# Two recurrent attention layers and two gated layers: per-head weight products formed on chip, and both layers advanced in one stream of segments

## The chip, the cores and the metric

The kernel runs on one core of one Trainium2 chip. The metric is the device time of one execution in microseconds, median of several runs; lower is better. The engines are PE (TensorE, matrix products), DVE (VectorE), ACT (ScalarE), POOL (GpSimd) and SP (which issues transfers); in the traces below each starts its instructions in the order in which the program put them there, and stands at one whose inputs or outputs are not free, whatever stands behind it.

## The reference, cut to what matters

```python
def A(x, mem0, Wq, Wk, Wv, Wo):            # 16 heads of 256, model width 448
    mem = mem0                              # 8 memory rows
    for s in range(64):                     # segments of 32 rows, one after the other
        h = concat([mem, x[32*s:32*s+32]])  # 40 rows
        q, k, v = h@Wq, h@Wk, h@Wv          # per head
        p = softmax(where(mask, q@k.T/16, -1e9))
        o = sum over heads of (p@v)@Wo
        mem = o[:8]                         # the next segment needs it
        outs.append(o[8:])

def B(x): return (relu(x@W_gate) * (x@W_up)) @ W_down      # 448 -> 1792 -> 448

x = x + A(layernorm(x)); x = x + B(layernorm(x))
x = x + A(layernorm(x)); x = x + B(layernorm(x))            # same weights again
```

Both attention layers use the same weights, and so do both gated layers (GLU below). Within a layer the memory makes segment s+1 wait for segment s. But layer 2's segment s needs only layer 1's segment s (and the GLU of it), so the two layers can run at the same time, some segments apart.

## The kernel before

It runs layer A, then B, then A, then B. In A, the projections of 128 ordinary rows (four segments) are computed ahead as filler; what depends on the memory is computed in each segment, 8 columns at a time:

```python
def step(self, s):                       # one segment of one layer
    # q and k of the 8 memory rows, after the previous segment's memory
    for qk in range(2):
        for blk in range(32):
            for kt in range(4):
                matmul(psA[:, c*8:c*8+8], lhsT=W[kt, blk], rhs=memT[kt])     # 128x128 by 128x8
    ...                                  # filler: projections of the next four segments
    for h in range(16): ...              # scores, softmax
    for r_ in range(2):                  # v of the memory rows: four column tiles side by side
        for jj in range(4):
            for kt in range(4):
                matmul(psO[r_][32*jj:32*jj+8, 0:512], lhsT=memT[kt], rhs=Wv[kt, chunk],
                       tile_position=(0, 32*jj))
    ...                                  # transposes of P, P@V, evictions
    for dc in range(4):                  # the new memory: 8 columns again
        for blk in range(32):
            matmul(psA[:, dc*8:dc*8+8], lhsT=Wo[blk, dc], rhs=OmT[blk])
```

## Time and profile before

| | |
|---|---|
| time | 4356 us |
| PE / DVE / ACT busy | 79% / 19% / 22% |
| mean granted PE clock | 0.71 |
| matmuls | 75,328, of them 49,152 of 8 columns |

The page's first part lists the busy time of each engine, its share of the span and its instructions; the fourth part follows the work that ended last back through whatever released each step.

```profile
PE 3462.1 (79%) x75328; PEld 2657.6 (61%) x75328; DVE 838.8 (19%) x2249; ACT 972.6 (22%) x2144; POOL 4.8 (0%) x8
...
PE 74%; DMA 8%; ACTq 8%; ACT 6%; DVE 2%; issue 2%; SPq 0%; DVEq 0%
```

PE is the bottleneck, and it is mostly busy. What with? The groups of PE instructions (line, operation, output and inputs, shapes and count | busy us, mean ns of one | idle before, and what ended it):

```profile
L726 PE MATMUL psA<-memT,Wqk_sb 128*128 128x8 bf16 x8192 | 875.9, 168 | 0.0
L594 PE MATMUL psB<-xnT,Wqk_sb 128*128 128x128 bf16 x2048 | 529.6, 259 | 0.0
L726 PE MATMUL psA<-memT,Wk_sb 128*128 128x8 bf16 x12288 | 452.7, 168 | 2.1 <-issue 2.0
L907 PE MATMUL psA<-arena,Wo_sb 128*128 128x8 bf16 x16384 | 449.4, 167 | 12.3 <-ACT arena L879 12.0 <-issue 0.3
L726 PE MATMUL psA<-memT,Wq_sb 128*128 128x8 bf16 x12288 | 448.5, 168 | 24.4 <-DVE memT L920 24.4
```

The groups of L726 and L907 have means of 167 or 168 ns, but these matmuls overlap in the pipeline: the cost of one is the spacing from one start to the next. In the windows view (us from the start; length, busy time and number, granted clock, transfers) 256 matmuls of 8 columns take 7.0 us and 128 of them 3.35 us, 26 to 27 ns each. The clock in the longer stream is half (0.50), yet one matmul costs nearly the same there as in the shorter one at full clock:

```profile
1002.19:1009.18 6.99, 6.99 (x257) 0.50 0.02 5
1022.96:1026.31 3.35, 3.35 (x130) 1.00 0.02 5
1077.78:1080.16 2.38, 2.38 (x39) 0.80 0.00 0
```

So an 8-column matmul costs about half of a 128-column one at full clock (16 of those take 1.06 us; less about 0.17 us until the last one's result is out, its drain, that is 55 ns each). The third window is the column-tiled V product: 32 matmuls of 512 columns in 2.4 us at clock 0.80. One after the other at that clock they would take about 8.8 us (an estimate: 4 x 55 ns each, divided by 0.80), so the four tiles run side by side. The Trainium skill ("TensorEngine Tiling (Array Packing)", Theoretical Speedup) gives up to 4 times for this, and the trace agrees with about 3.7 times.

Four segments of one layer take 116 us, 29 us a segment, 128 times; the two GLU stages take 257 and 251 us, loading 57 us.

### The profile page before, as it was taken

To read this page: it belongs to the slowest core of one execution; us is meant where nothing else is said; L and a number is where in the kernel's file an instruction comes from. 1 tells how busy PE (TensorE), PEld (TensorE's weight loads), DVE (VectorE), ACT (ScalarE), POOL (GpSimd) and SP (SyncE) were. 2 spreads that over 40 slices of the span, in tenths; PEclk is the share of its full clock that TensorE was granted. 3 is DMA by queue.
4 is the path that set the end of the run, shared out by engine and by line. 5 is a ranking of instruction groups with operands and counts; after the bars stand their busy time and mean duration, and the time that the engine had idled before them with its cause. 6 is when DMAs were issued, how large, how long until landed. Compare 5 with 4: busy or idle time off the path is not lost.

```text
span 4355.4 us, 157049 instructions
## 1 busy us (share of the span) xinstructions
PE 3462.1 (79%) x75328; PEld 2657.6 (61%) x75328; DVE 838.8 (19%) x2249; ACT 972.6 (22%) x2144; POOL 4.8 (0%) x8
## 2 busy tenths in 40 slices
PE   2888888888888888866668888888888888888567
PEld 2766666666666667642246666666666666666333
DVE  2111111111111111112221111111111111111132
ACT  1222222222222222212222222222222222221122
POOL 0000000000000000000000000000000000000000
PEclk8677677767776677667776667767777777676588
DMA  4000000000000000010010000000000000000100
GB/s 158 13 14 17 16 17 17 16 16 14 16 17 15 15 17 12 17 43 28 17 31 15 16 12 17 14 17 16 17 17 16 17 17 14 16 17 16 55 17 13
DMA packets 57597, 94.70 MB, mean 22 GB/s; under 512 B 13376, under 2 KB 49728, under 8 KB 51520
## 3 DMA queue, kind: packets, MB, share of 16 engines
q1 hardware_dynamic: 44672, 76.25, 6.7%
q10 hardware_dynamic: 12288, 8.40, 1.1%
q8 instruction: 590, 9.67, 0.9%
q14 instruction: 47, 0.39, 0.0%
HBM read 35.33 MB, written 7.34 MB: 10 GB/s over the span
## 4 chain that ended last, share of the span: by engine, by line
PE 74%; DMA 8%; ACTq 8%; ACT 6%; DVE 2%; issue 2%; SPq 0%; DVEq 0%
PE psA L726 20%; PE psB L594 12%; PE psA L907 10%; PE psO L777 8%; ACTq L805 8%; PE psB L661 6%; PE psB L624 5%; DMA xring<-out_dram 3%; PE psO L861 3%; PE psO L982 2%; PE psS L758 2%; ACT arena L801 2%; DMA arena<-arena 2%; PE psB L982 2%; DMA out_dram<-xring 1%
## 5 line engine op out<-in xcount | busy, mean ns | idle before, releaser
L726 PE MATMUL psA<-memT,Wqk_sb 128*128 128x8 bf16 x8192 | 875.9, 168 | 0.0
L726 PEld LDWEIGHTS psA<-memT,Wqk_sb 128*128 128x128 bf16 x8192 | 843.7, 103 | 0.4 <-issue 0.2
L594 PE MATMUL psB<-xnT,Wqk_sb 128*128 128x128 bf16 x2048 | 529.6, 259 | 0.0
L603 ACT ACTIVATE arena<-psB 128x512 bf16<-128x512 f32 x512 | 299.1, 596 | 838.1 <-PE psB L594 570.2
L726 PEld LDWEIGHTS psA<-memT,Wq_sb 128*128 128x128 bf16 x12288 | 446.3, 102 | 35.6 <-DVE memT L920 27.4
L726 PE MATMUL psA<-memT,Wq_sb 128*128 128x8 bf16 x12288 | 448.5, 168 | 24.4 <-DVE memT L920 24.4
L907 PEld LDWEIGHTS psA<-arena,Wo_sb 128*128 128x128 bf16 x16384 | 446.1, 101 | 25.5 <-ACT arena L879 16.5
L907 PE MATMUL psA<-arena,Wo_sb 128*128 128x8 bf16 x16384 | 449.4, 167 | 12.3 <-ACT arena L879 12.0
L726 PE MATMUL psA<-memT,Wk_sb 128*128 128x8 bf16 x12288 | 452.7, 168 | 2.1 <-issue 2.0
L726 PEld LDWEIGHTS psA<-memT,Wk_sb 128*128 128x128 bf16 x12288 | 444.1, 104 | 2.4 <-issue 2.4
L594 PE MATMUL psB<-xnT,Wq_sb 128*128 128x128 bf16 x3072 | 324.7, 253 | 111.4 <-ACT arena L603 74.6
L594 PE MATMUL psB<-xnT,Wk_sb 128*128 128x128 bf16 x3072 | 344.3, 262 | 72.6 <-ACT arena L603 72.6
L777 PE MATMUL psO<-Wv_sb,memT 128*8 128x512 bf16 x4096 | 365.6, 518 | 0.0
L624 PE MATMUL psB<-Wv_sb,xnT 128*128 128x512 bf16 x1024 | 292.0, 425 | 76.9 <-ACT arena L635 76.9
L594 PEld LDWEIGHTS psB<-xnT,Wq_sb 128*128 128x128 bf16 x3072 | 256.3, 115 | 146.1 <-ACT arena L603 79.7
L594 PEld LDWEIGHTS psB<-xnT,Wk_sb 128*128 128x128 bf16 x3072 | 269.8, 119 | 106.6 <-ACT arena L603 77.7
L737 ACT ACTIVATE arena<-psA 128x512 bf16<-128x512 f32 x128 | 76.4, 597 | 954.7 <-PE psA L726 954.7
L861 PE MATMUL psO<-arena 40*128 40x40 bf16 x4096 | 141.5, 188 | 153.4 <-DMA arena<-arena 153.4
L661 PE MATMUL psB<-Wo_sb,arena 128*128 128x448 bf16 x1024 | 249.2, 413 | 0.0
L594 PEld LDWEIGHTS psB<-xnT,Wqk_sb 128*128 128x128 bf16 x2048 | 245.8, 120 | 0.0
L861 PEld LDWEIGHTS psO<-arena 40*128 40x128 bf16 x4096 | 128.2, 100 | 180.4 <-issue 164.4
L777 PEld LDWEIGHTS psO<-Wv_sb,memT 128*8 128x8 bf16 x4096 | 128.1, 104 | 168.1 <-issue 138.1
(90 smaller groups left out, 2479.1 us busy)
## 6 DMA issues: line engine op xcount, KB each, us to landing
arena<-arena SPq DMA_DIRECT2D x128, 256.0 KB, 2.9
arena<-arena ACTq DMA_DIRECT2D x512, 16.0 KB
out_dram<-xring SPq DMA_DIRECT2D x64, 112.0 KB, 1.7
xring<-out_dram SPq DMA_DIRECT2D x64, 112.0 KB, 2.0
Wo_sb<-in_A_Wo_dram SPq DMA_DIRECT2D x1, 3584.0 KB, 36.1
xring<-in_A_x_dram SPq DMA_DIRECT2D x32, 112.0 KB, 1.9
arena<-in_B_W_down_dram SPq DMA_DIRECT2D x2, 1568.0 KB, 12.6
Wq_sb<-in_A_Wq_dram SPq DMA_DIRECT2D x3, 1024.0 KB, 9.4
```

What stands on the lines that cost most here:

```text
L594: r = sch.emit("pe", lambda E, ci=ci, kt=kt, lhsT=lhsT, rhs=rhs: E.matmul(ps[:, ci * 128:(ci + 1) * 128], lhsT=lhsT, rhs=rhs, start=(kt == ...
L603: te = sch.emit("act", lambda E: E.activation(dst, src, ACT.Copy), waits=[(ev_p, tl), qkt_wait_pe], inc=ev_a)
L624: r = sch.emit("pe", lambda E, kt=kt, lhsT=lhsT, rhs=rhs: E.matmul(ps[:, 0:512], lhsT=lhsT, rhs=rhs, start=(kt == 0), stop=(kt == 3)), wai ...
L661: r = sch.emit("pe", lambda E, blk=blk: E.matmul(ps[:, 0:D], lhsT=S.OsT[oi][:, blk, :], rhs=S.Wo_sb[:, blk, :], start=(blk == 0), stop=(bl ...
L726: r = sch.emit("pe", lambda E, c=c, kt=kt, lhsT=lhsT, rhs=rhs: E.matmul(S.psA[:, c * 8:c * 8 + 8], lhsT=lhsT, rhs=rhs, start=(kt == 0), st ...
L758: r = sch.emit("pe", lambda E, base=base, col=col, cq=cq, ck=ck, et=et: E.matmul(S.psS[base:base + L, col:col + L], lhsT=S.QKT[wi][:, cq, ...
L777: rr = sch.emit("pe", lambda E, r_=r_, jj=jj, kt=kt, lhsT=lhsT, rhs=rhs: E.matmul(S.psO[r_][32 * jj:32 * jj + 8, 0:512], lhsT=lhsT, rhs=rh ...
L801: te = sch.emit("act", lambda E, r_=r_: E.activation(S.vstage[0:104, r_, :], S.psO[r_][0:104, 0:512], ACT.Copy), waits=[(ev_p, t_vm[r_]), ...
L805: tvm = sch.emit("act", lambda E, jj=jj: E.dma_start(dstv[:, :, jj, :], S.vstage[32 * jj:32 * jj + 8, :, :]), waits=[(ev_a, t_vmev[1]), (e ...
L861: r = sch.emit("pe", lambda E, pi=pi, i=i, blk=blk, h=h: E.matmul(S.psO[pi][:, L * i:L * i + L], lhsT=S.Vbuf[vb][0:L, blk * 128:blk * 128 ...
L907: r = sch.emit("pe", lambda E, dc=dc, d0=d0, blk=blk: E.matmul(S.psA[:, dc * 8:dc * 8 + 8], lhsT=S.Wo_sb[:, blk, d0:d0 + 128], rhs=S.OmT[: ...
L982: r = sch.emit("pe", lambda E, ps=ps, kt=kt, lhsT=lhsT, rhs=rhs: E.matmul(ps[:, 0:ntok], lhsT=lhsT, rhs=rhs, start=(kt == 0), stop=(kt == 3)),
```

## The change

The intent: fold weights that are only ever used together. Scores are h (Wq Wk^T) h^T and the output is P h (Wv Wo), per head. M = Wq Wk^T and N = Wv Wo (448 x 448 per head) are formed once on chip. Then one product T = M h serves scores, V disappears (P multiplies h itself), and N is applied at the end. All 40 columns of a segment, memory and ordinary rows, go through T together, and layer 2's segment, four behind, joins them as 40 more columns. The GLU takes 64 rows of each layer as one tile of 128. Everything is issued in one loop of 68 steps, with `run_fill` putting the output product (even steps) or the GLU (odd steps) between the parts of the recurrence. The diff is a rewrite; its core, cut and shortened (names such as `m_nat` and `p_t_mem` stand for blocks of the kernel):

```diff
-for qk in range(2):                          # per segment and layer
-    for blk in range(32):
-        for kt in range(4): matmul(psA[:, 8 cols], W[kt, blk], memT[kt])
-... Q/K of four segments: 64 x 4 matmuls of 128 columns, V: 32 of 512
-for dc in range(4):
-    for blk in range(32): matmul(psA[:, 8 cols], Wo[blk, dc], OmT[blk])
+LAG = 4                                      # layer 2 is four segments behind
+def layers(t): return (0 if t < 64 else 1, 2 if t >= LAG else 1)
+# setup, once: transposes of Wq, Wk, Wv, then per head M = Wq Wk^T, N = Wv Wo
+def t_unit(t, k, r, eng):                    # 7 units of 8 blocks in each step
+    for j in range(8):
+        for kt in range(4):
+            MM(R[r][:, j, both layers], M[:, kt, 8*k+j, :], hT[kt, both layers])   # 80 columns
+    ...                                      # two evictions, on ACT or DVE in turn
+def un_mem(t):                               # memory rows of both layers times N
+    for k in range(14):
+        for j in range(4):                   # four column tiles
+            MM(b[32*j:32*j+32, 0:448], UTm[:, 14*j+k : 14*j+k+2], N[:, 14*j+k], ...)
+    hi = copy(b)  (ACT);  lo = b - hi  (DVE) # two bf16 halves of the new memory
+def ln_stats(...):                           # per layernorm
+    bn_stats, bn_aggr (DVE); Ln, Exp (ACT)
+def step(t):
+    side = [m_nat] + ([ln_b] if odd) + softmax ops of t-1 + [transposes of P]
+    for k in [6, 0, 1, 2, 3, 4, 5]:
+        t_unit(t, k, ...); two of side
+    fill = even: projections of t-1, then U N of the pair;  odd: GLU of the last pair
+    run_fill(500); s_mem(t); s_seg(t); run_fill(1500); p_t_mem; run_fill(400); u_mem
+    odd: rest of the GLU, then fill = projections of t-1, statistics of the next pair
+    un_mem(t); ...; run_fill(1200); m_t(t); ...; run_fill(rest)
```

## The prediction

> **What bounds the kernel now.** TensorE. The busy table gives PE 79% of 4355 us, DVE 19%, ACT 22%; the chain that ended last is 74% PE. Attention is 87% of the time: in the timeline four segments of one layer take 116 us, 29 us a segment, 128 times = 3.7 ms; two GLU stages about 0.5 ms; loading 57 us. Much of the PE work is tiny: 49,000 of 75,000 matmuls have 8 columns (256 for memory Q/K and 128 for the new memory per segment, 7.0 and 3.35 us, 26 ns each). In the windows view the clock is 0.50 inside the Q/K streams, 1.00 inside wide ones, mean 0.71; matmuls of 128 columns take 55 ns (16 in 1.05 us) at full clock, 107 at half. The Trainium skill ("TensorE: Matmul & The Clock Gate", Part 1) knows the states 4/8 and 8/8, chosen by how busy the array is; the trace agrees.
>
> **Removed, added.** Matmuls by the instruction order: 75,328 to about 31,000. Gone: the Q/K and V projections (4 + 256 + 32 per group), 384 8-column matmuls per segment, V staging DMAs, phase barriers. Added per step (both layers at once, 68 steps): 224 matmuls of 80 columns, 56 column-tiled of 448, about 75 small; per pair of steps 56 of 448 columns plus GLU 112 of 128 and 14 of 448. At full clock (55 ns per 128 columns; column tiling overlaps fourfold, 32 of 512 in 2.4 us): 8.0 + 2.8 + about 3.5, and 19.5/2 = 9.8 us: 24 us of PE per step, about 1.65 ms in all. Products on chip: transposes and evictions (0.6-1.1 us each), prologue about 115 us instead of 57.
>
> **Critical path.** PE will not be dense: in-order queues make new waits, summed with trace durations (evict 512: 0.69 DVE, 0.60 ACT; reduce/add 320: 0.49; stats 0.63; ACT table load 1.28):
> - odd steps: the GLU's layernorm sits after 34 matmuls of the step; statistics plus Ln and Exp, each with its table load, 3.1 us on ACT, stall PE about 6 us.
> - odd steps, end: the next layernorm's Ln/Exp and loads stand before the hi copy of the new memory on ACT; then lo, projection evictions, transposes: about 6-7 us stall.
> - transpose of P, first PSUM bank after the last T unit, hB before the down projection, U before the output product: 1-2.5 us each.
> Even step about 31 us, odd about 42, 73 per pair; 34 pairs, the first and last two lighter, is 2.45 ms. Plus prologue and tail. Stalls over 3 us also drop the clock. DVE work is about 16 us, ACT 13 us per step.
>
> **Predicted: 2560 us**, 80% range 2230 to 2880. Faster by over 2%: 0.98; within 2%: 0.01; slower: 0.01.
>
> **What would show it.** About 31,000 matmuls; PE busy 60-75%; T matmuls the costliest group, 36 ns each; mean clock 0.8-0.95; table loads about 136; PE idle before the GLU transposes (bG<-xn) near 6 us per pair released by DVE's normalisation; DVE about 45% and ACT about 35% busy; a pair of steps at 73 us, odd longer than even; T start after prologue near 115 us.
>
> **What would make it wrong.** If stalls keep the clock at half, T units cost 67 ns per matmul and the time nears 3 ms. If 80-column streams count as busy and the waits overlap more than my serial sum, 2.2 ms. If column-tiled 448-column matmuls do not overlap, +7 us per step, 0.5 ms.

## The result, and the profile after

The changed kernel takes 2521.5 us (2515.6 to 2522.3, 4 runs), the kernel before 4356.5; the ratio is 0.578 (95% interval 0.577 to 0.579). Ratios here are the mean time of one kernel's runs over that of the other's of the same rounds, so not quite the ratio of the medians quoted. The predicted time was 2560, 1.5% off. It computes the reference.

Busy times and the chain of the changed kernel:

```profile
PE 1940.4 (77%) x30924; PEld 1399.6 (56%) x30924; DVE 1074.5 (43%) x2630; ACT 861.8 (34%) x1859; POOL 94.3 (4%) x160
...
PE 59%; DVE 24%; ACT 13%; issue 4%; POOL 0%; DVEq 0%; ACTq 0%; POOLq 0%
```

PE's share of the span hardly changed, but the chain did: 37% of it is DVE and ACT, where it was 8%. The groups:

```profile
L126 PE MATMUL R<-hT,Mw 128*128 128x80 bf16 (+1 forms) x15232 | 653.5, 212 | 45.2 <-issue 23.1
...
L126 PE MATMUL bO<-Nw,big 128*128 128x448 bf16 x1904 | 437.9, 386 | 62.5 <-DVE big L294 61.2
...
L126 PE MATMUL bC<-Nw,UTm 128*32 128x448 bf16 x3752 | 194.6, 359 | 1.4 <-DVE UTm L294 1.4
L126 PE MATMUL bG<-ident,xn 128*128 128x128 bf16 x272 | 39.4, 297 | 193.8 <-DVE xn L507 193.8
```

The last line is 68 sets of four small transposes with 194 us of idle PE before them: nearly all of it is the GLU's layernorm, once per odd step. One even step, one odd step and the pair, in the windows view (columns: length, busy time and count of PE, PEld, DVE, ACT and POOL, PE clock, transfers):

```profile
1362.82:1395.73 32.91, 28.56 (x411) 18.80 (x412) 11.78 (x29) 7.87 (x20) 0.00 (x0) 0.90 0.01 1
1395.73:1434.53 38.80, 27.02 (x491) 21.64 (x490) 18.84 (x45) 16.40 (x33) 2.22 (x4) 0.86 0.02 5
1362.82:1434.53 71.71, 55.59 (x901) 40.44 (x902) 30.62 (x74) 24.28 (x53) 2.22 (x4) 0.88 0.01 3
```

A pair of steps moves both layers on by two segments each, with all their GLU work, in 71.7 us. The kernel before needed 4 x 29 us for the attention alone. 16 us of the pair PE is idle. Adding up PE's gaps of over 0.2 us over the steady steps: 4.4 us in an even step (1.9 before the output product, 1.5 before the transposes of P, 0.95 before the projections), 11.9 in an odd one (5.7 before the GLU's transposes, 3.1 before the late projections, 0.6 to 0.9 in four other places).

The longest of these in the timeline (start us, length, engine, line, operation, count; in brackets the idle time before it and what ended it):

```profile
1324.01 1.31 PE L126 MATMUL R<-hT,Mw 128*128 128x80 bf16 x32
1324.21 0.62 DVE L780 TENSOR_TENSOR XB<-bO,XA 128x448 bf16<-128x448 f32 x1 [4.40 <-PE bO L126]
...
1326.94 0.63 DVE L496 BATCH_NORM_STATS2 stat<-XB 128x6 f32<-128x448 bf16 x1
1327.00 0.54 ACT L292 ACTIVATE hK<-bC 8x448 bf16<-8x448 f32 x1 [0.89 <-DVE hK L294]
1327.56 1.28 ACT L498 ACT_TABLE_LOAD   x1
1327.60 0.18 DVE L497 BATCH_NORM_AGGREGATE stat<-stat 128x2 f32<-128x6 f32 x1
1328.85 0.29 ACT L498 ACTIVATE stat<-stat,cvec 128x1 f32<-128x1 f32 x1
1329.17 1.28 ACT L500 ACT_TABLE_LOAD   x1
1330.46 0.20 ACT L500 ACTIVATE stat<-stat 128x1 f32<-128x1 f32 x1
1330.77 0.61 DVE L507 TENSOR_SCALAR xn<-XB,stat 128x448 bf16<-128x448 bf16 x2 [2.98 <-ACT stat L500]
...
1331.43 0.61 PE L126 MATMUL bG<-ident,xn 128*128 128x128 bf16 x4 [5.73 <-DVE xn L507]
```

PE has 192 more T matmuls of this step to run, but the transposes stand before them in its queue. They wait for DVE's normalisation, that for ACT's Exp, that for a table load, Ln, another table load and DVE's statistics.

### The profile page after: what moved, and what is told of

The parts are those of the page before. It is cut to its first block, busy times and chain, and to the rows that moved or that the text cites. A ratio compares the mean times of both kernels' runs of the same rounds, so it can differ in the third digit from the quotient of the medians.

```text
span 2520.5 us, 67762 instructions
## 1 busy us (share of the span) xinstructions
PE 1940.4 (77%) x30924; PEld 1399.6 (56%) x30924; DVE 1074.5 (43%) x2630; ACT 861.8 (34%) x1859; POOL 94.3 (4%) x160
## 4 chain that ended last, share of the span: by engine, by line
PE 59%; DVE 24%; ACT 13%; issue 4%; POOL 0%; DVEq 0%; ACTq 0%; POOLq 0%
PE R L126 28%; PE bO L126 21%; PE bC L126 6%; DVE big L294 5%; DVE TTs L294 4%; ACT L500 3%; PE bG L126 3%; ACT TTs L292 2%; ACT L498 2%; DVE xn L507 2%; DVE TTm L294 1%; DVE hK L294 1%; DVE hB L800 1%; DVE stat L657 1%; DVE Ps L659 1%
## 5 line engine op out<-in xcount | busy, mean ns | idle before, releaser
L126 PE MATMUL R<-hT,Mw 128*128 128x80 bf16 (+1 forms) x15232 | 653.5, 212 | 45.2 <-issue 23.1
L126 PEld LDWEIGHTS R<-hT,Mw 128*128 128x128 bf16 x15232 | 639.3, 108 | 76.2 <-issue 38.6
L126 PE MATMUL bO<-Nw,big 128*128 128x448 bf16 x1904 | 437.9, 386 | 62.5 <-DVE big L294 61.2
L126 PEld LDWEIGHTS bO<-Nw,big 128*128 128x128 bf16 x1904 | 188.0, 105 | 260.7 <-DVE big L294 67.2
L126 PE MATMUL R<-xBT,big 128*128 128x128 bf16 x3808 | 232.7, 220 | 28.2 <-ACT TTs L292 27.5
L126 PEld LDWEIGHTS R<-xBT,big 128*128 128x128 bf16 x3808 | 215.9, 98 | 33.9 <-ACT TTs L292 31.8
L126 PE MATMUL bC<-Nw,UTm 128*32 128x448 bf16 x3752 | 194.6, 359 | 1.4 <-DVE UTm L294 1.4
L126 PE MATMUL bG<-ident,xn 128*128 128x128 bf16 x272 | 39.4, 297 | 193.8 <-DVE xn L507 193.8
L294 DVE CAST TTs<-R 128x512 bf16<-128x512 f32 (+3 forms) x272 | 177.0, 651 | 0.0
L294 DVE CAST big<-R 128x512 bf16<-128x512 f32 (+1 forms) x256 | 146.9, 618 | 53.7 <-PE R L126 50.8
L292 ACT ACTIVATE TTs<-R 128x512 bf16<-128x512 f32 (+3 forms) x272 | 153.2, 563 | 0.0
```

The costliest lines, as they stand in the source:

```text
L126: ins = E.matmul(out, lhsT=lhsT, rhs=rhs, **kw)
L292: self.sc.op("act", lambda E: E.activation(out, src, ACT.Copy), reads, writes)
L294: self.sc.op(eng, lambda E: E.tensor_copy(out, src), reads, writes)
```

## The experiments

Eight kernels ran; all of them computed the reference. Ratios are to the kernel before (the changed kernel: 0.578).

### 1. The products without the common stream (e1_no_stream)

```diff
-LAG = 4
+LAG = 64          # layer 2 starts when layer 1 has ended; its input goes through DRAM
```

(with the loads and stores that this needs). The per-head products, T, U and N, the column tiling and all orders stay; each of 128 steps now has one layer in it.

> Products kept, but layer 2 is 64 segments behind instead of 4 (its input goes through DRAM), so the layers run one after the other: 128 steps of one layer instead of 68 of mostly two. Theory A (my prediction's arithmetic: a step costs almost the same for one layer as for two, since T falls only from 36 to about 25 ns a matmul and the waits stay): the one-layer steps at the end of the changed kernel's trace take 31 us, so about 128 x 32 + 170 = 4250 us, range 4000 to 4600: the gain is nearly all lost. Rival B (the products are the gain, fewer matmuls per layer): well below, 3000 to 3500 us.

It took 3945 us, ratio 0.906: below theory A's range (layer 1's steps took 30.7 us on average and layer 2's 28.9, not 32), and far above rival B's. So of the 1835 us that the change took off, the products and the new shape of a step bring 410 alone, and running both layers at once 1425. Why it is so much is in the page's first line of this run, and in 96 T matmuls of 40 columns in its timeline (first line of the second block) against 96 of 80 in that of the changed kernel (second line):

```profile
PE 3185.3 (81%) x54316; PEld 2200.5 (56%) x54316; DVE 1485.4 (38%) x4429; ACT 1259.5 (32%) x3057; POOL 161.7 (4%) x280
```

```profile
1261.38 2.56 PE L126 MATMUL R<-hT,Mw 128*128 128x40 bf16 x96
...
1371.24 3.60 PE L126 MATMUL R<-hT,Mw 128*128 128x80 bf16 x96
```

1245 of the 1425 us are PE busy time, at nearly the same mean clock (0.875 here, 0.879 there). A T matmul of 40 columns (less the drain: 25 ns) costs two thirds of one of 80 (36 ns); and the output product and the GLU multiply a tile of 128 rows whether 64 or 128 of them mean something. Sharing work, more than filling waits, is what the stream does. In this form: a kernel with one layer at a time could fill those tiles with 128 rows of its own layer, so 410 us may not be all that the products can bring alone; that was not tried.

### 2. One table set for Ln and Exp (e2_one_table)

```diff
 def _(eng):
+    eng.preload_act_table_set("natural_log_exp_and_others")
     for f in ops["act"]: f(eng)
```

The Trainium skill ("ScalarE: Activation LUTs", Table sets: the hidden batching unit) says that one named set holds both functions, so that Ln followed by Exp needs one load. The trace of the changed kernel shows that this does not come by itself: both the Ln and the Exp of each of 68 layernorms have a load of 1283 ns.

> One line: a table set that holds both Ln and Exp is loaded once, so 136 table loads of 1.28 us go. Theory A (the layernorm chains of the odd steps hold PE, tables are 2.56 us of each): PE idle before the GLU's transposes 5.7 to about 3.2 us per pair, idle before the late projections 3.1 to about 1 us, 4.5 to 5 us per pair, 2340 to 2380 us. Rival B (ACT is 34% busy, its loads are hidden, DVE's chain sets the wait): under 1 us per pair, 2490 to 2520.

It took 2398 us, ratio 0.551, with one load left. This lies between the two theories' numbers, nearer to A. The idle before the GLU's transposes fell from 5.7 to 3.4 us a pair, as expected (117.0 us in all, from 193.8):

```profile
L126 PE MATMUL bG<-ident,xn 128*128 128x128 bf16 x272 | 32.2, 253 | 117.0 <-DVE xn L508 117.0
```

The idle before the late projections fell only from 3.1 to 2.1, not to 1. The timeline of the changed kernel says why: there the first of the two loads runs long before its input is there, at 1350.59, while ACT waits for DVE's statistics until 1356.27, so only the second load was on that path.

```profile
1350.59 1.28 ACT L498 ACT_TABLE_LOAD   x1
...
1356.05 0.18 DVE L497 BATCH_NORM_AGGREGATE stat<-stat 128x2 f32<-128x6 f32 x1
1356.27 0.29 ACT L498 ACTIVATE stat<-stat,cvec 128x1 f32<-128x1 f32 x1 [4.39 <-DVE stat L497]
1356.58 1.28 ACT L500 ACT_TABLE_LOAD   x1
...
1357.88 0.20 ACT L500 ACTIVATE stat<-stat 128x1 f32<-128x1 f32 x1
1357.98 0.53 ACT L712 ACTIVATE hi<-bC 128x448 bf16<-128x448 f32 x1
```

### 3. The GLU's transposes later on PE (e3_lnb_late)

```diff
-side = [m_nat, ln_b (statistics, apply, transposes), softmax ops, seg_pt]
+side = [m_nat, ln_b (statistics, apply), softmax ops, seg_pt, ln_b_t (transposes)]
```

> Only the GLU layernorm's transposes are moved on PE from after 34 matmuls to after the transposes of P; its Ln and Exp with the loads stay where they are. Theory A (the early place in PE's order is the cause): idle before these transposes 5.7 to under 0.5 us; ACT still stands 3 us in the loads while T waits for evictions, so 2.5 to 5 us per pair come back, 2350 to 2440 us. Rival B (the next wait, transposes of P or T's banks, takes all of it): 2490 to 2520.

It took 2466 us, ratio 0.566: 56 us less, outside both ranges. The idle before the transposes went to 0.5 us as theory A said, but PE then stood before the third T unit instead:

```profile
L126 PE MATMUL R<-hT,Mw 128*128 128x80 bf16 (+1 forms) x15232 | 667.2, 214 | 185.3 <-DVE TTs L294 141.2 <-issue 22.8 <-ACT hT L292 13.6
```

T's second bank is emptied by DVE, and that eviction stands behind the normalisation in DVE's queue, which still waits for ACT's Exp. Taking the wait off PE's queue moved it to DVE's: T's own idle rose from 0.7 to 5.0 us a pair of steps.

### 4. Both (e4_table_late)

> Both. Theory A: the two causes overlap only in the GLU chain, so 5.7 plus about 2 us per pair less, 2230 to 2290 us, mean clock above 0.90 [...]. Rival B (what one of them leaves hides the other): no better than the better of the two alone.

It took 2346 us, ratio 0.539, not the 2230 to 2290 of theory A. The saving of 176 us is about the sum of the two alone (123 and 56). It is better than either alone, so rival B is out too. T still waits 2.8 us in each pair of steps: 68.9 us in all are ended by the same eviction on DVE, which now stands behind a shorter chain.

```profile
L126 PE MATMUL R<-hT,Mw 128*128 128x80 bf16 (+1 forms) x15232 | 622.9, 207 | 116.9 <-DVE TTs L295 68.9 <-ACT hT L293 23.8 <-issue 23.1
```

### 5. The memory's output product without column tiles (e5_no_coltile)

```diff
-for k in range(14):
-    for j in range(4):
-        MM(b[32*j:32*j+32, 0:D], UTm[:, 14*j+k : 14*j+k+2], N[:, 14*j+k], ...)
+for o in range(56):
+    MM(b[0:16, 0:D], UTm[:, o], N[:, o], start=(o == 0), stop=(o == 55))
```

(with the selection matrices to match: one block of rows instead of four).

> The output product of the memory rows runs as 56 matmuls of 16 stationary columns one after another in one column tile instead of four tiles side by side (same result). Theory A (tiles overlap fourfold and the product lies on the chain of every step): 56 x 189 ns = 10.6 us instead of 2.8, about 7.5 us more in each of 67 steps, 3000 to 3060 us. Rival B (tiles hardly overlapped, or the product hides under waits): under 2700 us.

It took 3008 us, ratio 0.690: 487 us more, 7.3 us in each of 67 steps, as theory A had it. The 56 matmuls take 2.83 us in four tiles (the changed kernel's timeline, first line) and 10.76 us in one (this run's):

```profile
1386.69 2.83 PE L126 MATMUL bC<-Nw,UTm 128*32 128x448 bf16 x56
...
1646.43 10.76 PE L126 MATMUL bC<-Nw,UTm 128*16 128x448 bf16 x56
```

Of the 7.9 us that the product became longer, 7.3 show in the step, so hardly any of it vanishes in waits elsewhere. At 487 us the column tiling of this one product is worth more than the waits that runs 2 to 4 removed (176 us).

### 6. Order alone (e6_order)

On top of run 4, no instruction is added or removed. What moved, and the one dependency that was loosened (last line):

```diff
 def step(t):
-    side: two per T unit, in the order m_nat, ln_b, softmax, seg_pt
+    odd:  [m_nat] [statistics, reduce] [Ln/Exp, subtract] [exp, sum, apply] [1/x, P] [seg_pt, ln_b_t] []
+    even: [m_nat, reduce] [subtract, exp] [sum, 1/x] [P] [] [seg_pt] []     # one list per T unit
-    run_fill(500); s_mem(t)
+    s_mem(t); run_fill(500)
+    odd: two projections before the last of the down projection, not after un_mem
+    odd: statistics and apply of the next pair both before un_mem's hi and lo; run_fill(300), not 1200, after un_mem
-un_units: each waits for all of U                     # a dependency, not only an order
+un_units: each waits only for the chunk of U that it reads
```

> On top of one table and late transposes only the order in which work is put into the in-order queues changes: GLU statistics, Ln/Exp and normalisation spread over the T units, transposes of P one or two units later, the memory's scores before the first projection, two late projections before the end of the down projection, the next normalisation before hi/lo, the output product waiting only for the chunk of U it reads. Theory A (the remaining idle of PE, about 12 us a pair, is mostly order): T's bank wait 2.8 to under 1, late projections 2.2 to under 0.7, U 1.9 to under 0.5, P 2.2 to about 1: 6 to 7 us per pair, 2100 to 2170 us. Rival B (DVE's 16 us per step and the serial chain set the pace): over 2280 us.

It took 2076 us, ratio 0.476, a little better than theory A and the fastest of all. Against run 4, which it builds on, that is 269 us or 11.5% less; against the changed kernel 445 us, but 176 of these are run 4's. The page and one pair of steps:

```profile
PE 1823.2 (88%) x30924; PEld 1315.8 (63%) x30924; DVE 1065.9 (51%) x2630; ACT 689.1 (33%) x1723; POOL 94.3 (5%) x160
```

```profile
1130.81:1158.89 28.08, 25.90 (x411) 17.27 (x412) 11.79 (x30) 8.18 (x21) 0.26 (x1) 1.00 0.01 2
1158.89:1188.26 29.37, 25.26 (x491) 19.93 (x490) 18.42 (x45) 11.00 (x28) 1.96 (x4) 0.99 0.03 6
1130.81:1188.26 57.45, 51.16 (x901) 37.20 (x902) 30.20 (x75) 19.17 (x49) 2.23 (x5) 0.99 0.02 4
```

Set against the changed kernel's pair (so with run 4's part in it), matmuls and DVE work are the same; 14.3 us are gone, of them about 10 us idle PE and 4.4 us of PE busy time, the same matmuls at clock 0.99 instead of 0.88. DVE with the same work as before does not hold the kernel above 2280 us, as rival B had it. In the odd step shown T waits 0.3 us in all, the wait of the late projections is gone, and 1.8 us now stand before the selection of the new memory (it waits for lo). The moves were made together; which of them brought how much is not shown.

### 7. Useless matmuls in the wait (e7_keep_warm)

Runs 2 to 6 mix two effects: a changed amount of waiting, and a higher clock (0.90 to 0.97, from 0.88). This run adds work to the changed kernel to separate them.

```diff
+    # odd steps, after m_nat, before ln_b: into a bank that the next T unit overwrites
+    for j in range(96): MM(R[1][...], M[:, 0, j % 8, :], hT[0, both layers], start=True, stop=True)
```

> The changed kernel with 96 useless 80-column matmuls (3.4 us) put into PE's idle 5.7 us before the GLU's transposes in odd steps. Theory A (the idle drops the clock to half for 3 us afterwards and that costs about 1.5 us a pair): clock 0.50 after the wait becomes 1.00 and the time falls by 30 to 60 us, to 2460 to 2490. Rival B (after the wait DVE and ACT set the pace, PE's clock does not matter there): 2510 to 2530.

It took 2514 us, ratio 0.576. The number fits rival B, but the run did not do what it was made for: the windows after the useless matmuls show that the clock fell to 0.50 all the same, as soon as the transposes came. So it says nothing about what the half clock costs.

```profile
1395.78:1397.78 2.00, 1.13 (x32) 1.00 (x28) 0.00 (x0) 1.97 (x3) 0.00 (x0) 1.00 0.03 8
1397.78:1399.78 2.00, 0.58 (x12) 0.58 (x13) 0.61 (x2) 0.79 (x3) 0.00 (x0) 0.97 0.00 0
1399.78:1401.78 2.00, 2.00 (x34) 2.00 (x32) 0.15 (x1) 0.46 (x1) 0.00 (x0) 0.50 0.00 0
```

The gap left was 2.3 us. The Trainium skill ("TensorE: Matmul & The Clock Gate", the table at its end) asks for no gaps over about 3 us; here 2.3 us was already too long. So was less: in an even step of the changed kernel the 1.92 us before the output product (from 1306.29 to 1308.21) ended in the half clock too, and the clock records of the whole trace show it after each of the 32 waits of this length (and after 1 of the 31 of 1.5 us). A wait of 0.95 us comes 2.3 us before each of them and may count too, so no threshold is shown. The idle before the GLU's transposes is therefore only one of several that cost clock.

```profile
1306.00:1308.00 2.00, 0.29 (x6) 0.10 (x4) 1.60 (x6) 1.03 (x3) 0.00 (x0) 0.98 0.00 0
1308.00:1310.00 2.00, 1.79 (x5) 0.74 (x6) 0.15 (x1) 0.00 (x0) 0.00 (x0) 0.50 0.00 0
```

### 8. The wait filled nearly whole (e8_fill_wait)

```diff
-    for j in range(96): MM(...)
+    for j in range(152): MM(...)
```

> The run before left 2.3 us of the wait empty, and the clock still fell to 0.50 right after it, so it did not test the cost of the half clock. Now 152 useless 80-column matmuls (5.5 us) fill the wait nearly whole. Both theories: idle before the GLU's transposes under 0.4 us and the clock 1.00 in the 4 us after them. Theory A (the half clock after the wait costs): the 128 T matmuls after it take about 5 instead of 6.3 us, 1 to 1.6 us a pair, 35 to 55 us, about 2470 us. Rival B (T's bank evictions and the softmax on DVE set the pace there): within 15 us of 2514, the fall already seen.

It took 2476 us, ratio 0.568: with 5.5 us of useless work in each odd step the kernel is 46 us faster. The clock stayed at 1.00, and the 128 T matmuls after the transposes took 4.76 us (the last line is the changed kernel's, for comparison):

```profile
1372.20 5.61 PE L126 MATMUL R<-hT,Mw 128*128 128x80 bf16 x152
1378.09 0.40 PE L126 MATMUL bG<-ident,xn 128*128 128x128 bf16 x4 [0.29 <-DVE xn L507]
1378.33 4.76 PE L126 MATMUL R<-hT,Mw 128*128 128x80 bf16 x128
...
1331.83 6.34 PE L126 MATMUL R<-hT,Mw 128*128 128x80 bf16 x128
```

In the changed kernel the same 128 took 6.34 us, 1.6 more, and 46 us over 33 odd steps is 1.4 us a step. Theory A holds: the half clock after this wait costs about 1.4 us, on top of whatever the 5.7 us of the wait itself cost (this run leaves that in place, filled with useless work).

## Why the prediction was right, point by point

- **The time.** 2560 against 2521.5. The sum it was made of, 73 us per pair of steps, was 71.7; but the two parts of it, work and waits, were each wrong, in opposite ways: too little busy time by 7.6 us, too much idle by 9. That the total came within 1.5% is luck; the mechanism, in-order queues whose waits add up beside PE's work, is not. "24 us of PE per step", 48 a pair, was 55.6 busy. About 3 us of the difference is work that I sized too low at full clock (run 6, at clock 0.99, has 51.2 in a pair), and 4.4 is the half clock after the waits, which the prediction named as a danger ("If stalls keep the clock at half") but did not put into its sum; run 8 priced the one after the longest wait at about 1.4 us a pair. For the idle part the sum held 25 us a pair, and 16 were measured.
- **"About 6-7 us stall" at the end of odd steps** was the single wait that was mis-sized most: 3.8 us, 3.1 before the late projections and 0.7 before T. I had put the layernorm's two table loads one after the other on the path to hi. One of them runs while ACT waits for its input anyway (run 2's timeline), and PE works on the memory's output product and the first late projections meanwhile.
- **"Stall PE about 6 us" before the GLU's transposes**: 5.7, by the chain that was named. Runs 2, 3, 7 and 8 act on this wait: the loads in it, its place on PE, and what fills it.
- **The other waits, "1-2.5 us each"**: 1.9, 1.5 and 0.95 in even steps, 0.6 to 0.9 in odd ones; in the right places, but smaller. The 25 us of idle leave some 12 for them (an estimate: 25 less 6 and 6.5), and they add up to 6.7 us a pair; most of the 9 us too many lie here.
- **Even 31, odd 42 us**: 32.9 and 38.8; odd is the longer one, but by half of what was said, for the reasons above.
- **The signs.** Matmuls 30,924 (said: about 31,000), T the costliest group (653.5 us) at 36 ns each where the clock is full, clock 0.88 (0.8 to 0.95), table loads 137 (136), DVE 43% and ACT 34% busy (45, 35), T starts at 110.7 us (115). PE's busy share of 77% is above the 60 to 75% that was said.
- **"If column-tiled 448-column matmuls do not overlap, +7 us per step, 0.5 ms"**: they do overlap; run 5 took the overlap away, and it cost 7.3 us a step, 0.49 ms.
- **Not predicted**: how the gain divides. Run 1 shows that products and a new step without the common stream are worth 410 us, and the stream 1425. This is one order of undoing; the stream without the products was not tried, and what it would be worth stays open.

## What to carry to other kernels

When PE is 80% busy with small matmuls, count what each costs against its columns: here 8 columns cost 26 ns, 40 cost 25 and 80 cost 36, so one product for two independent recurrences side by side costs 36 ns where two cost 50 (and the whole kernel 1940 us of busy PE where run 1 has 3185). After such a rewrite look at the order in the in-order queues: list the waits of the bottleneck engine, and move whole chains, because a wait taken off one queue can turn up in the next (run 3); reordering all queues together brought another 11.5% with the same instructions (run 6 against run 4). A wait on PE can also cost the slower clock after it (run 8: about 1.4 us after a wait of 5.7).

## What the Trainium skill lacked or had wrong

- "TensorE: Matmul & The Clock Gate", Part 1, describes the clock by busy and idle windows of about 3.4 us, and its table at the end allows gaps up to about 3 us. Here a gap of 2.3 us brought the half clock (run 7), though PE had been busy without a break for over 13 us before it; so did one of 1.9 us with one of 0.95 us shortly before it (the changed kernel's even steps), and one of 0.3 us did not (run 8). Part 1 does say that frequent short idles make the clock swing, but gives no length for them.
- The same page says only of transposes (Part 4) that they do not bring the full clock. 256 matmuls of 8 columns, back to back for 7.0 us in the kernel before, ran at 0.50 too, with PE busy in all of it; why is not shown. So of the prediction's "the trace agrees" the two states are shown, and that how busy PE is decides between them is not.
- "ScalarE: Activation LUTs", Table sets, says that Ln followed by Exp needs one table load. In the changed kernel it had two per layernorm (136 in all) until the common set was loaded by name, and the page, whose rules say to use that set, does not say that it must be asked for; then one load was left in the whole kernel, and 123 us were saved (run 2).
- The same page, What ACT_TABLE_LOAD costs, adds about 1380 ns of drain to the load's 1283. The load's 1.28 us is as in the trace; the drain is not seen there: the load at 1327.56 us ended at 1328.84, and Ln ran at 1328.85.
- The same page does not say that a load can run ahead of the wait of its activation: at 1350.59 it did, 5.7 us before the Ln that it served, and so that load cost no time there.
